# The same steps in another order: a hand-written order of windowed attention and a gated feed-forward block

## The chip, the core and the metric

The kernel runs on one core of a Trainium2 chip. The core has a matrix engine (TensorE, PE in the profile), three engines for element-wise work (VectorE, DVE; ScalarE, ACT; GpSimd, POOL), and SyncE (SP), which issues transfers. Each engine works through its own queue in the order in which the program gave it work, and waits for other engines by semaphores. PE writes only into PSUM, eight banks of 128 partitions by 2 KB; ACT and DVE read the banks. Transfers between device memory and on-chip memory are issued from the queues of SP, ACT and POOL. The metric is the device time of one execution in microseconds, us.

## What is computed

Attention over 4 batches of 8 heads, 768 positions and 64 values a head, with a window of 96 positions, 8 global keys and a bias that falls with the distance; its output, as 3072 tokens of 512 values, goes through a gated feed-forward block of width 1536:

```python
scores = scale * np.matmul(q, k.transpose(0, 1, 3, 2))
keep = is_global | is_local
bias = -slopes[:, None, None] * dist[None, :, :]
scores = np.where(keep, scores + bias[None], -1000000000.0)
a = np.exp(scores - scores.max(-1, keepdims=True))
attn = np.matmul(a / a.sum(-1, keepdims=True), v)
x = attn.transpose(0, 2, 1, 3).reshape(3072, 512)
g, val = x @ w_gate, x @ w_val
out = (g / (1 + np.exp(-g)) * val) @ w_out
```

## The kernel before

The work is cut into 1092 small steps. A step is a call of one short function, written as a name and numbers, and the string ORDER (line 37) lists all of them in the order in which they are given to the engines. Nothing else sets the order: the loop on lines 667 to 669 takes one step after the other. As every engine has a queue of its own, the place of a step in ORDER decides two things: what stands ahead of it on its own engine, and which of the eight PSUM banks it gets. The functions `single` and `double` (lines 236 and 226) deal out one bank or two neighbouring banks, from a list in which `release` puts a bank at the end when, in program order, its last reader has been given out. A product that gets a bank waits on the chip until that last reader is done.

The attention of a batch b is done for pairs of heads hp (four pairs), in units u of the keys, each 120 keys wide plus the 8 global keys. Tokens go in tiles t of 384, two to a batch; the feed-forward block takes its width in 12 blocks f of 128. The names:

| step | engine | what it does (line) |
|---|---|---|
| Lf, Ld, Li | ACT or SP | load the first queries (Lf.A) and keys (Lf.S) as 32-bit numbers, the table of distances, the identity (253 to 259) |
| Lh, Lv, LG, L4, Lr, Lw, Lo | POOL | load other queries and keys, values, global values, stages of later batches, the three weights (263 to 320) |
| cast | A, V or P | the first queries and keys to 16 bits (352) |
| T, U | PE | transposes of queries (last number 1) and keys (0) of batch 0 and of batch 1 (369, 407) |
| k, q; kw, qw | A or V | copy the transposed keys and queries of batch 0 and 1 out of PSUM (382, 398; 415, 425); k and kw end with a small copy of the global keys on DVE (388, 419) |
| sl, M | DVE, ACT | the slopes times the identity (334); exp of the biases as masks (340) |
| B, c, x, m | PE, PE, ACT, DVE | the bias written into PSUM (466), scores (479), exp (489), mask (508). In batch 0 a unit gets either B ahead of c or m behind x |
| w | PE | weighted values; the last number is 0 for the denominators, 1 and 2 for the numerators (540) |
| i, r, p, n | DVE, DVE, DVE, ACT | reciprocal of the denominators, its spreading, the scaled x, the numerators out of PSUM (556, 563, 573, 549) |
| g, v | PE | the products with w_gate and w_val, four matmuls of 384 columns (590); ga and gb are the two halves of a g |
| t, s, h | ACT, DVE, DVE | tanh of half the gate, (1 + tanh) times the gate, times the value (596, 600, 606) |
| o, e | PE, ACT | the product with w_out in parts of three matmuls (631), and its way out (649), with the store issued by SP |
| D, K | SP, DVE | transposes by DMA of queries and keys of batches 2 and 3 and of half of batch 1 (435), keys into their blocks (442 to 445) |
| G, Z | V, P or S | copies of the global values, a cleared tail (282, 280, 285) |

A last letter V, A, P or S names the engine. T.3.0.1 is the transpose of the queries of head pair 3, first half; w.0.0.0.2 is batch 0, heads 0 to 3, first half, second numerator. For batch 1, hp 0 and 1 are transposed on PE (U, then kw and qw), the rest by DMA.

The second gate of waits is the buffers: two staging buffers each for keys and for queries, two for DMA-transposed keys, two for the output rows.

Of the kernel before, what the change touches and what calls it, by code (L numbers as in the profile page):

```python
# [60 lines left out]
x.1.1.1 h.1.1 o.0.0.0 v.1.11 g.1.9 v.1.9 s.1.5 v.1.5 g.1.7 t.1.7 g.1.3 t.1.9 Lr.1.1.6 m.1.0.1.V  # L61
D.1.2.1 m.1.0.0.V h.1.5 Lv.1.3 D.1.3.0 o.0.1.0 g.1.11 o.0.0.1 Lv.1.2 o.0.1.1 t.1.3 o.0.0.2 s.1.7
Lr.3.0.1 Lr.2.0.5 v.1.0 m.1.1.1.V o.0.1.2 o.0.1.3 D.1.3.1 t.1.11 s.1.9 s.1.3 s.1.11 o.0.0.3 h.1.0
v.1.3 h.1.11 m.1.1.0.V w.1.0.0.0 h.1.9 Lv.2.2 Lr.2.1.0 K.1.2 i.1.0.0 e.0.1 w.1.0.0.1 Lr.2.0.4 e.0.0
w.1.0.0.2 c.1.2.1 h.1.3 c.1.2.0 r.1.0.0 n.1.0.0 o.0.2.0 Lr.2.1.4 D.2.0.0 K.1.3 x.1.2.1 p.1.0.0.0.V
x.1.2.0 o.0.2.1 Lv.1.5 o.1.0.0 c.1.3.0 c.1.3.1 m.1.2.1.V c.1.0.2 o.0.2.2 o.1.0.1 x.1.3.0 m.1.3.0.V
# [638 lines left out]
```

## Time and profile before

| | before |
|---|---|
| runs | 239.68, 239.74, 240.7 us; median 239.74 |
| profiled execution | 239.84 us |
| its span (first to last instruction) | 238.0 us |
| PE busy | 231.6 us, 97% of the span |
| DVE busy | 171.7 us, 72% |
| ACT busy | 117.5 us, 49% |
| POOL busy | 78.2 us, 33%, all of it in the first 112 us |
| granted TensorE clock | 1.00 |

What lies around the span is 239.84 - 238.0 = 1.84 us. In rows of the timeline the first number is the start in us from the span's start, the second the length of the merged instructions, then the engine (with q: its sequencer, which issues and waits), the line, the operation, what it writes and reads, and how many were merged; in brackets stands the idle time of the engine just before and what ended it. In groups by line the numbers after the bar are busy time in us, the mean of one in ns, and the idle time before. A matmul's end is modelled, so the busy time of PE holds waits; where PE stands still is read from the distance between starts.

### The profile page before, as it was taken

Reading aid. Unit: us, or ns where it says so; the run is one execution under the profiler, and the core shown is the slowest. Engines: PE = TensorE matmul, PEld = TensorE weight load, DVE = VectorE, ACT = ScalarE, POOL = GpSimd, SP = SyncE. Lnnn points to the kernel's source line nnn. Section 1 sums busy time; section 2 is a strip of 40 time slices with the busy share of each in tenths; the row PEclk is TensorE's granted clock in tenths of the full one; section 3 lists DMA queues with packets and bytes.
Section 4 is the critical chain, followed back from the end, with each engine's and each line's share of the span. In section 5 each row is a group of like instructions: output and inputs, shape, how many; then the busy total and the mean of one; then the engine's idle time right before and its main releaser. Section 6 shows DMA issues by size and latency. Waiting matters only on the chain.

```text
span 238.0 us, 5798 instructions
## 1 busy us (share of the span) xinstructions
PE 231.6 (97%) x2356; PEld 133.7 (56%) x2356; DVE 171.7 (72%) x411; ACT 117.5 (49%) x218; POOL 78.2 (33%) x99
## 2 busy tenths in 40 slices
PE   6999999999999999999999999999999999999994
PEld 4566566554556555555655654665555655555452
DVE  3799999767799976877948879889548854755400
ACT  3799813943776336377543366632453414223111
POOL 8874896720799845776000000000000000000000
PEclk9999999999999999999999999999999999999999
DMA  7999999999999999999974060100020101100114
GB/s 167 177 185 206 192 194 177 183 183 135 182 145 155 151 148 148 168 167 128 134 113 104 30 86 17 74 3 0 3 88 0 47 4 48 41 0 27 64 45 176
DMA packets 88715, 25.56 MB, mean 107 GB/s; under 512 B 78536, under 2 KB 85744, under 8 KB 88688
## 3 DMA queue, kind: packets, MB, share of 16 engines
q0 software_dynamic: 67520, 13.81, 70.9%
q1 hardware_dynamic: 20480, 10.80, 24.1%
q10 hardware_dynamic: 688, 0.59, 0.7%
q8 instruction: 18, 0.29, 0.6%
q14 instruction: 9, 0.07, 0.1%
HBM read 28.58 MB, written 6.29 MB: 146 GB/s over the span
## 4 chain that ended last, share of the span: by engine, by line
PE 89%; DMA 4%; ACT 3%; DVE 1%; issue 0%; SPq 0%; DVEq 0%; ACTq 0%
PE banks L590 52%; PE banks L631 25%; PE banks L540 5%; PE banks L479 4%; ACT at L489 2%; DMA dist<-dist_c 2%; DMA kN<-kst 2%; PE banks L620 1%; PE banks L466 1%; PE banks L369 1%; PE banks L407 1%; DVE xT L573 0%; DVE rb L563 0%; ACT masks L340 0%; ACT qT L398 0%
## 5 line engine op out<-in xcount | busy, mean ns | idle before, releaser
L596 ACT ACTIVATE th<-banks 128x384 f32<-128x384 f32 x96 | 44.7, 493 | 71.1 <-PE banks L590 68.0
L590 PE MATMUL banks<-xT,wv 128*128 128x384 f16 x384 | 72.7, 326 | 0.1
L590 PE MATMUL banks<-xT,wg 128*128 128x384 f16 x384 | 72.3, 326 | 0.1
L631 PE MATMUL banks<-wo,hT 128*128 128x512 f16 x276 | 68.0, 379 | 0.3 <-DVE sl L600 0.3
L606 DVE TENSOR_TENSOR hT<-banks,sl 128x384 f16<-128x384 f32 x96 | 51.5, 552 | 20.9 <-PE banks L590 19.5
L600 DVE SCALAR_TENSOR_TENSOR sl<-th,banks 128x384 f32<-128x384 f32 x96 | 50.3, 546 | 16.5 <-ACT th L596 15.7
L590 PEld LDWEIGHTS <-wv 128*128 128x128 f16 x384 | 37.1, 98 | 27.8 <-issue 0.7
L590 PEld LDWEIGHTS <-wg 128*128 128x128 f16 x384 | 36.8, 98 | 26.3 <-issue 0.3
L489 ACT ACTIVATE at<-banks 128x864 f16<-128x864 f32 (+2 forms) x52 | 42.1, 842 | 9.2 <-PE banks L479 8.6
L631 PEld LDWEIGHTS <-hT 128*128 128x128 f16 x276 | 26.1, 98 | 27.5 <-issue 1.5
L508 DVE TENSOR_TENSOR at<-at,masks 128x864 f16<-128x864 f16 (+3 forms) x60 | 25.5, 470 | 3.9 <-ACT at L489 3.7
L267 POOL DMA_DIRECT2D vS<-in_v_dram x28 | 25.4, 914 | 7.0 <-DMA vS<-in_v_dram 2.3
L649 ACT ACTIVATE osb<-banks 128x512 f32<-128x512 f32 x23 | 13.5, 598 | 25.0 <-PE banks L631 23.4
L308 POOL DMA_DIRECT2D kst<-in_k_dram x20 | 17.1, 855 | 16.7 <-PE banks L540 12.1
L308 POOL DMA_DIRECT2D qst<-in_q_dram x20 | 17.0, 858 | 3.6 <-DMA wo<-in_moe_w_out_dram 1.0
L479 PE MATMUL banks<-qT,kT 64*128 64x216 f16 (+5 forms) x240 | 14.4, 240 | 0.0
L573 DVE TENSOR_TENSOR xT<-ns,rb 128x384 f16<-128x384 f32 x24 | 12.6, 548 | 0.1
L479 PEld LDWEIGHTS <-kT 64*128 64x128 f16 x240 | 8.3, 94 | 7.4 <-issue 5.9
L540 PE MATMUL banks<-at,vS 128*32 128x216 f16 (+6 forms) x576 | 12.0, 225 | 0.4 <-issue 0.4
L549 ACT COPY ns<-banks 128x768 f32<-128x768 f32 x12 | 9.6, 799 | 4.8 <-PE banks L540 4.7
L540 PEld LDWEIGHTS <-vS 128*32 128x32 f16 x576 | 9.8, 95 | 2.6 <-issue 2.2
L556 DVE STREAM_TRANSPOSE dT<-banks 128x384 f32<-128x384 f32 x16 | 9.2, 575 | 1.4 <-PE banks L540 1.2
(59 smaller groups left out, 116.5 us busy)
## 6 DMA issues: line engine op xcount, KB each, us to landing
out_dram<-osb SPq DMA_DIRECT2D x23, 256.0 KB, 2.2
vS<-in_v_dram POOLq DMA_DIRECT2D x24, 120.0 KB, 7.6
qst<-in_q_dram POOLq DMA_DIRECT2D x20, 96.0 KB, 8.1
kst<-in_k_dram POOLq DMA_DIRECT2D x20, 96.0 KB, 7.4
wg<-in_moe_w_gate_dram POOLq DMA_DIRECT2D x6, 256.0 KB, 9.2
wv<-in_moe_w_val_dram POOLq DMA_DIRECT2D x6, 256.0 KB, 8.9
wo<-in_moe_w_out_dram POOLq DMA_DIRECT2D x3, 512.0 KB, 8.6
q<-in_q_dram POOLq DMA_DIRECT2D x3, 192.0 KB, 7.0
```

Of the source, the lines that this page charges most:

```text
L267: nc.gpsimd.dma_start(out=v_of(b)[NG:NG + n, c, :, :], in_=v[b, :, KC * c:KC * c + n, :].rearrange("h p d -> p h d"))
L308: nc.gpsimd.dma_start(out=rows_of(i, b, h // 2)[:, :, h % 2, :], in_=KQ[i][b, h].rearrange("(t p) d -> p t d", p=128))
L479: nc.tensor.matmul(sc[:, hi, col:col + n], lhsT=kTs[hp][r, 128 * c:128 * c + 128], rhs=qTs[b, hp][r, q0:q0 + n], start=fresh, stop=True, s ...
L489: nc.scalar.activation(out=at[:, :, 0:w], in_=scs.pop((b, hp, u))[:, :, 0:w], func=AF.Exp, scale=scale)
L508: ENG[e].tensor_mul(a2, a2, m[:, :, m0:m0 + n])
L540: nc.tensor.matmul(dst[r, o:o + n], lhsT=vSs[b][:, c, 4 * g + j, what - 1::2] if what else ones[:, 0:32], rhs=ats[b, hp, u][:, j % 2, col: ...
L590: nc.tensor.matmul(gv[t, f, which][:, 0:TB], lhsT=w[:, c, 128 * f:128 * f + 128], rhs=xTs[t][:, c, :], start=(c == 0), stop=(c == NC - 1))
L596: nc.scalar.activation(out=th, in_=gv[t, f, 0][:, 0:TB], func=AF.Tanh, scale=0.5)
L600: nc.vector.scalar_tensor_tensor(out=sl, in0=gv[t, f, "t"], scalar=1.0, in1=gv[t, f, 0][:, 0:TB], op0=AluOp.add, op1=AluOp.mult)
L606: nc.vector.tensor_mul(hTs[t][:, f, :], gv[t, f, 1][:, 0:TB], gv[t, f, "s"])
L631: nc.tensor.matmul(ops_t[t, i], lhsT=hTs[t][:, f, 128 * i:128 * i + 128], rhs=wo[:, f, :], start=(f == 0), stop=(f == NFF - 1))
L649: nc.scalar.mul(out=osb, in_=ops, mul=0.5)
```

## The change

All 1092 steps stay, but for six, which change their engine or their unit:

| before | after | |
|---|---|---|
| cast.0.1.A | cast.0.1.V | first keys of head pair 1: ACT to DVE |
| cast.0.0.A | cast.0.0.P | first keys of head pair 0: ACT to POOL |
| kw.0.V | kw.0.A | keys of batch 1, pair 0: DVE to ACT |
| qw.1.V | qw.1.A | queries of batch 1, pair 1: DVE to ACT |
| B.0.1 | B.0.2 | bias by PE for unit 2 in place of unit 1 |
| m.0.0.2.V | m.0.0.1.V | mask by DVE for unit 1 in place of unit 2 |

All others stand at another place. The table of distances (Ld.S) is first on SP's queue, ahead of the identity and the keys. Ten of the sixteen mask steps M stand at the head of ACT's queue, ahead of the first copy (before, they stood among the exps). The casts of the keys leave ACT. On POOL's queue cast.0.0.P stands between the loads Lh.1.1.0.4 and Lh.0.1.0.4, and Z.0.P and G.0.4.7.P stand earlier. On PE's queue T.3.0.1 and T.2.0.1 stand ahead of the first scores, T.3.1.0 stands ahead of w.0.0.0.2, and the four U of batch 1 are followed by five v, with all four copies out of their banks on ACT. The steps of later batches are mixed anew; among them K.3.3, before the last of the four K.3, comes first.

The diff is one hunk, 89 lines against 89, and only ORDER differs. Its first fourteen lines on each side, and those around the places that the prediction speaks of:

```diff
@@ -35,89 +35,89 @@
 ORDER = """
-Lf.A.1.1 Lf.S.0.1 LG pre cast.1.1.V fill.14 Li T.1.0.1 Lf.A.1.0 sl.3 cast.0.1.A sl.2 T.1.0.0 Ld.S
-B.1.0 Lf.S.0.0 B.1.1 k.1.0.V Lh.1.0.4.8 sl.1 cast.1.0.V fill.2 q.1.0.V cast.0.0.A sl.0 sl.6 sl.5
-T.0.0.1 c.0.1.1 T.0.0.0 c.0.1.0 M.3.1 T.3.0.1 T.2.0.1 q.0.0.A x.0.1.1 B.0.0 Lh.0.0.4.8 k.0.0.V B.0.1
-sl.4 c.0.0.1 sl.7 q.3.0.V M.5.1 Lv.0.2 M.0.1 Lh.1.1.0.4 Lv.0.0 x.0.1.0 c.0.0.0 q.2.0.V T.2.0.0
-x.0.0.1 T.3.0.0 k.2.0.V B.3.0 M.2.1 B.2.0 x.0.0.0 c.0.2.0 Lh.0.1.0.4 B.2.1 M.1.1 k.3.0.V w.0.0.0.0
-c.0.3.0 x.0.2.0 T.1.1.0 Z.2.V Lh.1.1.4.8 T.1.1.1 c.0.2.1 x.0.3.0 G.0.1.4.V i.0.0.0 q.1.1.V T.0.1.1
-B.3.1 c.0.3.1 T.0.1.0 Lv.0.3 k.1.1.A q.0.1.V k.0.1.V Lv.0.1 Lh.0.1.4.8 x.0.2.1 r.0.0.0 Lw.0.0.0
-T.3.1.1 T.2.1.1 x.0.3.1 q.3.1.A c.0.1.3 c.0.0.2 w.0.1.0.0 i.0.1.0 Lw.0.0.1 q.2.1.A w.0.0.0.1
-Lw.1.0.1 x.0.0.2 w.0.0.0.2 Lw.1.0.0 c.0.0.3 Lw.0.1.1 T.3.1.0 Lw.0.1.0 p.0.0.0.1.V r.0.1.0 T.2.1.0
-Lw.1.1.0 x.0.1.3 x.0.0.3 Z.0.P p.0.0.0.0.V w.0.1.0.1 p.0.1.0.0.V w.0.1.0.2 p.0.1.0.1.V k.3.1.A
-Lw.1.1.1 c.0.1.2 k.2.1.A ga.0.2 Lv.0.6 ga.0.0 ga.0.1 c.0.2.2 x.0.1.2 gb.0.0 m.0.0.2.V M.7.1 gb.0.1
-Lw.0.2.0 x.0.2.2 t.0.0 m.0.1.3.V m.0.1.2.V g.0.3 t.0.1 Lw.0.2.1 M.1.0 gb.0.2 m.0.0.3.V c.0.3.3 t.0.3
-c.0.3.2 s.0.0 t.0.2 Lv.0.5 s.0.1 w.0.0.1.0 v.0.0 M.4.1 s.0.3 s.0.2 v.0.2 v.0.3 h.0.0 M.5.0 M.6.1
-h.0.2 Lv.0.4 v.0.1 m.0.2.2.V x.0.3.3 Lw.1.2.1 c.0.2.3 x.0.3.2 x.0.2.3 M.2.0 g.0.7 m.0.3.3.V i.0.0.1
...
-Lr.1.1.7 m.0.3.2.V v.0.5 v.0.7 r.0.0.1 v.0.4 g.0.9 t.0.6 t.0.5 s.0.7 s.0.5 s.0.6 L4.1.0 h.0.5 Z.3.P
...
-t.1.1 g.1.2 s.0.10 v.1.8 g.1.4 h.0.4 h.0.10 s.0.8 s.1.1 U.0.0 U.1.1 t.1.8 U.0.1 U.1.0 t.1.2 s.1.8
-Lo.1 qw.0.A s.1.2 Lr.1.0.5 Lr.1.1.5 g.1.6 M.4.0 h.1.8 v.0.9 kw.0.V qw.1.V M.6.0 M.7.0 v.1.2 g.1.0
-kw.1.A h.0.9 h.1.2 t.1.4 v.1.6 M.0.0 t.1.6 c.1.0.1 t.1.0 s.1.4 s.1.6 c.1.1.0 x.1.1.0 D.1.2.0 Z.1.V
-g.1.5 G.1.0.7.S v.1.4 s.1.0 t.1.5 x.1.0.1 v.0.8 h.1.4 h.1.6 c.1.0.0 c.1.1.1 Lo.2 h.0.8 v.1.1 x.1.0.0
...
-w.2.1.1.0 w.2.1.1.2 i.2.0.1 c.3.1.1 c.3.0.1 D.3.3.0 o.3.2.0 i.2.1.1 x.3.0.1 K.3.2 g.4.7 n.2.1.1
-o.3.2.1 K.3.3 t.4.7 v.4.1 r.2.1.1 s.4.7 x.3.1.1 v.4.7 c.3.0.0 D.3.2.1 c.3.1.0 h.4.7 h.4.1 o.3.0.0
...
+Lf.A.1.1 Ld.S Lf.A.1.0 M.2.0 pre Li cast.1.1.V sl.0 sl.2 LG Lh.1.0.4.8 Lf.S.0.1 M.3.1 fill.14 sl.4
+M.6.0 sl.5 Lh.0.0.4.8 Lf.S.0.0 Lv.0.0 T.1.0.1 cast.0.1.V M.2.1 sl.3 B.1.1 Lh.1.1.0.4 cast.0.0.P
+q.1.0.V T.1.0.0 cast.1.0.V M.5.1 B.1.0 Lh.0.1.0.4 Z.0.P M.1.0 M.0.1 M.4.0 fill.2 sl.1 T.0.0.1 M.1.1
+M.7.1 T.0.0.0 k.1.0.V sl.7 Lv.0.3 k.0.0.V q.0.0.A M.5.0 T.3.0.1 T.2.0.1 c.0.1.1 Lh.1.1.4.8 Lv.0.2
+c.0.1.0 B.0.0 q.2.0.V q.3.0.V T.2.0.0 x.0.1.1 x.0.1.0 c.0.0.1 c.0.0.0 T.3.0.0 x.0.0.1 k.2.0.V B.2.0
+Lv.0.1 B.2.1 x.0.0.0 Lh.0.1.4.8 c.0.2.1 c.0.2.0 x.0.2.0 M.0.0 x.0.2.1 Lw.0.0.0 M.7.0 M.6.1 T.1.1.1
+k.3.0.V m.0.0.1.V sl.6 Lw.0.0.1 q.1.1.V T.0.1.1 T.0.1.0 Z.1.V Lw.1.0.1 k.0.1.V Lw.1.0.0 T.1.1.0
+B.3.0 c.0.3.0 B.3.1 Lw.0.1.0 c.0.3.1 x.0.3.0 q.0.1.V w.0.0.0.0 x.0.3.1 T.2.1.1 B.0.2 Lw.0.1.1
+G.0.1.4.V G.0.4.7.P k.1.1.A Lv.0.6 Lw.1.1.0 w.0.1.0.0 i.0.0.0 i.0.1.0 c.0.0.2 r.0.0.0 q.2.1.A
+c.0.1.3 w.0.0.0.1 T.3.1.1 x.0.0.2 T.3.1.0 x.0.1.3 r.0.1.0 k.3.1.A c.0.0.3 p.0.0.0.0.V w.0.0.0.2
+w.0.1.0.1 p.0.0.0.1.V p.0.1.0.0.V w.0.1.0.2 Lw.1.1.1 x.0.0.3 T.2.1.0 q.3.1.A ga.0.1 c.0.1.2
+p.0.1.0.1.V ga.0.2 ga.0.0 Lw.0.2.0 x.0.1.2 gb.0.2 m.0.1.3.V gb.0.0 m.0.0.3.V k.2.1.A t.0.2 m.0.1.2.V
+gb.0.1 t.0.0 c.0.2.2 c.0.3.2 Lw.0.2.1 s.0.2 x.0.2.2 w.0.0.1.0 s.0.0 t.0.1 g.0.3 v.0.0 Lv.0.5 x.0.3.2
+t.0.3 i.0.0.1 s.0.1 h.0.0 M.4.1 c.0.3.3 c.0.2.3 v.0.2 x.0.2.3 Lv.0.4 x.0.3.3 r.0.0.1 Lw.1.2.0 v.0.1
+g.0.5 g.0.6 g.0.4 h.0.2 g.0.7 v.0.5 Lw.1.2.1 m.0.2.2.V t.0.6 Lr.1.1.4 s.0.3 h.0.1 m.0.2.3.V v.0.3
+t.0.5 v.0.7 L4.1.0 m.0.3.3.V s.0.5 L4.0.0 Lv.1.2 v.0.6 m.0.3.2.V h.0.5 s.0.6 g.0.9 Lo.1 Lr.2.0.1
...
+s.0.11 g.1.1 h.0.4 D.1.2.0 s.0.10 g.1.0 t.0.8 v.0.11 g.1.8 s.0.9 U.1.1 h.0.10 Z.2.V s.0.8 t.1.2
+U.0.0 U.1.0 s.1.2 U.0.1 Lr.1.0.6 h.0.11 v.1.1 t.1.1 s.1.1 v.1.8 t.1.0 G.1.0.7.S t.1.8 qw.0.A
+Lr.1.0.7 D.1.2.1 v.1.0 kw.1.A Lr.1.1.7 qw.1.A h.1.1 s.1.8 D.1.3.0 Lr.3.0.1 v.1.2 kw.0.A v.0.8 h.1.8
+Lv.1.5 Lr.2.1.3 g.1.6 Lr.2.1.1 g.1.5 h.1.2 s.1.0 c.1.1.0 h.0.8 t.1.6 c.1.0.1 g.1.4 x.1.1.0 s.1.6
...
+t.4.6 s.4.3 h.3.11 o.2.1.2 s.4.6 t.4.4 m.2.2.2.V g.4.5 v.3.9 g.4.2 g.4.10 v.4.6 h.3.9 K.3.3 g.4.1
...
 """
```

More of the change, by code (lines that the diff above doesn't have):

```diff
@@ L61 @@
[L61 to L66, printed above, removed]
@@ new lines @@
+i.1.1.0 o.1.0.1 r.1.1.0 Lr.2.1.5 n.1.1.0 Lr.2.0.7 o.1.0.2 x.1.0.2 D.2.1.0 Lr.2.1.4 Lr.2.1.6 x.1.3.2
+c.1.2.2 c.1.1.2 v.1.10 p.1.1.0.0.V p.1.1.0.1.V K.2.0 h.1.10 g.2.0 g.2.7 m.1.0.2.V g.2.6 D.2.2.0
+x.1.2.2 x.1.1.2 t.2.0 Lr.3.0.3 g.2.3 o.1.0.3 t.2.6 g.2.5 s.2.0 t.2.7 Lr.2.1.7 D.2.0.1 m.1.3.2.V
+s.2.6 t.2.5 v.2.6 m.1.2.2.V s.2.7 e.1.0 m.1.1.2.V s.2.5 v.2.0 w.1.1.1.0 w.1.1.1.1 D.2.1.1 Lv.2.3
+t.2.3 s.2.3 w.1.1.1.2 Z.3.P w.1.0.1.2 n.1.1.1 i.1.1.1 w.1.0.1.0 w.1.0.1.1 n.1.0.1 g.2.10 i.1.0.1
+v.2.3 g.2.2 v.2.2 t.2.2 h.2.3 h.2.6 D.2.2.1 h.2.0 g.2.1 t.2.10 Lv.3.1 Lv.2.0 g.2.9 o.1.1.0 Lr.3.1.1
@@ new lines @@
+s.3.1 Lv.3.6 Lv.3.3 Lr.3.0.4 v.3.0 g.3.0 v.2.8 t.3.0 h.3.8 g.3.5 s.3.7 h.2.8 s.3.0 c.2.1.0 c.2.0.2
+D.3.3.0 t.3.5 x.2.1.0 v.3.7 s.3.5 x.2.0.2 h.3.0 v.3.3 h.3.7 g.3.9 c.2.1.1 h.3.3 m.2.1.0.V c.2.2.1
+c.2.2.0 o.2.2.0 x.2.2.0 K.2.3 m.2.0.1.V t.3.9 o.2.2.1 D.3.1.0 v.3.5 x.2.1.1 s.3.9 D.3.0.1 m.2.2.0.V
+Lv.3.4 x.2.2.1 g.3.10 g.3.4 c.2.3.1 t.3.4 c.2.3.0 x.2.3.1 h.3.5 s.3.4 m.2.2.1.V g.3.11 o.2.2.2
+o.2.0.0 m.2.1.1.V x.2.3.0 t.3.11 Lr.3.0.0 o.2.0.1 t.3.10 m.2.3.0.V g.3.2 o.2.2.3 v.3.1 s.3.11 t.3.2
+m.2.3.1.V e.2.2 w.2.1.0.2 s.3.2 w.2.1.0.1 w.2.0.0.0 w.2.1.0.0 h.3.1 w.2.0.0.1 w.2.0.0.2 n.2.1.0
@@ new lines @@
+h.4.0 h.4.5 v.4.3 v.4.2 s.4.2 w.2.1.1.1 w.2.1.1.2 e.3.1 h.4.3 s.4.8 h.4.2 K.3.0 w.2.1.1.0 w.2.0.1.2
+D.3.1.1 n.2.1.1 w.2.0.1.1 w.2.0.1.0 c.3.0.0 K.3.2 o.3.2.0 n.2.0.1 x.3.0.0 i.2.0.1 g.4.7 t.4.7
+i.2.1.1 c.3.0.1 c.3.1.0 r.2.1.1 c.3.1.1 s.4.7 p.2.1.1.1.V o.3.2.1 r.2.0.1 x.3.1.1 x.3.0.1 x.3.1.0
+o.3.2.2 o.3.0.0 o.3.2.3 m.3.1.1.V m.3.0.1.V e.3.2 p.2.0.1.0.V o.3.0.1 c.3.3.0 c.3.2.1 c.3.2.0
+o.3.0.2 G.3.0.7.S Lv.3.0 m.3.0.0.V x.3.2.0 p.2.1.1.0.V Lv.3.2 v.4.1 p.2.0.1.1.V v.4.10 v.4.7 x.3.2.1
+h.4.1 m.3.1.0.V g.4.11 w.3.0.0.2 x.3.3.0 h.4.10 t.4.11 m.3.2.1.V w.3.0.0.1 c.3.3.1 m.3.3.0.V x.3.3.1
@@ new lines @@
+o.3.0.3 n.3.0.0 g.5.10 g.5.0 v.4.8 m.3.2.0.V m.3.3.1.V t.5.10 g.4.9 e.3.0 s.4.11 g.5.11 t.5.0 s.5.10
+s.5.0 t.4.9 t.5.11 h.4.8 h.4.7 g.5.3 t.5.3 v.5.10 h.5.10 s.4.9 w.3.1.0.2 w.3.1.0.1 w.3.0.0.0
+w.3.1.0.0 g.5.7 v.5.0 n.3.1.0 g.5.4 i.3.0.0 v.4.11 g.5.2 s.5.11 i.3.1.0 h.5.0 h.4.11 t.5.7 s.5.3
+v.5.3 r.3.1.0 v.5.7 g.5.9 s.5.7 t.5.2 s.5.2 g.5.8 o.4.2.0 h.5.3 v.5.11 v.4.9 t.5.4 t.5.9 h.5.7 v.5.2
+v.5.9 r.3.0.0 t.5.8 p.3.1.0.0.V s.5.9 s.5.8 h.4.9 o.4.2.1 o.4.2.2 s.5.4 g.5.1 p.3.0.0.0.V
+p.3.0.0.1.V h.5.11 t.5.1 o.4.2.3 h.5.9 g.5.6 e.4.2 p.3.1.0.1.V t.5.6 h.5.2 c.3.0.2 c.3.1.2 x.3.0.2
@@ L121 @@
+h.7.10 v.7.3 o.5.0.1 o.6.2.0 o.6.0.2 h.7.5 o.6.0.3 t.7.8 s.7.3 v.7.11 o.5.0.2 h.7.3 o.6.1.3 o.7.0.0
+e.6.0 v.7.6 s.7.8 v.7.8 o.5.0.3 h.7.11 v.7.7 h.7.6 h.7.7 o.7.0.1 e.5.0 o.6.2.1 o.7.1.0 h.7.8 o.7.2.0
+o.6.2.2 e.6.1 o.7.0.2 o.6.2.3 e.6.2 o.7.0.3 e.7.0 o.7.2.1 o.7.1.1 o.7.1.2 o.7.1.3 o.7.2.2 e.7.2
+o.7.2.3 e.7.1 e.7.3
 """
```

90 lines of the change are left out of this document (34 added, 56 removed).

## The prediction

> **What bounds the kernel now.** The page came first. Lines of its parts 1 and 2:
>
> ```profile
> span 238.0 us, 5798 instructions
> PE 231.6 (97%) x2356; PEld 133.7 (56%) x2356; DVE 171.7 (72%) x411; ACT 117.5 (49%) x218; POOL 78.2 (33%) x99
> PE   6999999999999999999999999999999999999994
> DMA  7999999999999999999974060100020101100114
> ```
>
> PE has work from the first us to the last, at a granted clock of 1.00. The reader is to see two things: only the waits of PE can be shortened, since its work stays; and the transfers fill their engines for the first half of the span, so what a load has ahead of it sets when it lands. Second came the waits of PE: none that it lists behind the first 20 us is over 0.3 us. So, third, I took the distances between starts from the timeline, and the end of PE from the chain of waits (start, length, what):
>
> ```profile
> 1.19 3.17 PE L348 MATMUL banks<-ones 128*128 128x256 f16 x14 [1.19 <-DVE ones L326]
> ...
> 42.58 1.46 PE L590 MATMUL banks<-xT,wv 128*128 128x384 f16 x8
> 43.88 0.81 PE L590 MATMUL banks<-xT,wg 128*128 128x384 f16 x4
> 44.69 0.81 PE L590 MATMUL banks<-xT,wv 128*128 128x384 f16 x4
> 45.43 0.54 PE L479 MATMUL banks<-qT,kT 64*128 64x216 f16 x8
> ...
> 233.85 0.68 PE banks L620 x12
> ```
>
> From 42.58 to 43.88 eight matmuls of 384 columns take 1.30 us: 0.1625 each, 0.42 ns a column, 0.65 for one g or v. From 43.88 to 44.69 four take 0.81 instead of 0.65, so a wait of 0.16 sits in a stretch that the page calls busy. From 44.69 to 45.43 four take 0.74: the 0.09 over 0.65 is the change from matmuls on the whole array to those on part of it. With 0.42 ns a column (the small matmuls side by side) and 0.09 a change, the PE work of the old order adds up to 228.4 us. It ran from 1.19 to 233.85 + 0.68 = 234.53, 233.3 us. So all that a better order could win is 4.9 us: 4.2 before the first g, 0.7 behind it.
>
> **The change part by part.**
>
> *PE's own work.* The steps are the same but for B.0.2 in place of B.0.1: 192 more columns, 0.08 us. Changes of the array's shape, counted in the two orders: 86 before, 87 after, 0.09. Together +0.17, with no cover, since PE is the bound.
>
> *The start.* Rows of the timeline of before, then two groups by shape, then two lines of the page's part 6 (KB each, median us to landing):
>
> ```profile
> 0.74 0.46 SPq L259 DMA_DIRECT2D k<-in_k_dram  x1
> 1.75 0.43 SPq L256 DMA_DIRECT2D dist<-dist_c  x1
> 3.91 0.51 ACT L352 CAST k<-k 128x384 f16<-128x384 f32 x1 [0.83 <-DMA k<-in_k_dram]
> 2.17 0.79 POOL L263 DMA_DIRECT2D q<-in_q_dram  x1
> 4.65 0.77 POOL L263 DMA_DIRECT2D q<-in_q_dram  x1
> 6.34 0.86 POOL L263 DMA_DIRECT2D k<-in_k_dram  x1
> 7.20 0.51 ACT L352 CAST k<-k 128x384 f16<-128x384 f32 x1 [2.78 <-DMA k<-in_k_dram]
> 8.51 0.46 ACT L489 ACTIVATE at<-banks 128x336 f16<-128x336 f32 x1
> 9.21 0.84 PE L369 MATMUL banks<-ident,q 128*64 128x128 f16 x12
> 10.07 0.78 POOL L263 DMA_DIRECT2D k<-in_k_dram  x1
> 17.87 0.56 DVE L573 TENSOR_TENSOR xT<-banks,rb 128x384 f16<-128x384 f32 x1 [0.38 <-ACT at L489]
> 19.41 1.14 PE L590 MATMUL banks<-xT,wg 128*128 128x384 f16 x6
> ...
> L340 ACT ACTIVATE masks<-dist 128x432 f16<-128x432 f16 x8 | 4.5, 574 | 0.0
> L340 ACT ACTIVATE masks<-dist 128x216 f16<-128x216 f16 x8 | 2.9, 386 | 0.0
> ...
> q<-in_q_dram POOLq DMA_DIRECT2D x3, 192.0 KB, 7.0
> k<-in_k_dram POOLq DMA_DIRECT2D x3, 192.0 KB, 7.2
> ```
>
> ACT sits idle for 2.78 us ahead of the second cast. Ten masks move into such idle time; six long and four short, 6 x 4.5/8 + 4 x 2.9/8 = 4.8 us, from about 4 on. But the keys of pair 1 change places with the table on SP, first issue against third: they landed at 3.9, the time at which the first cast could start, and now land near 6. And the first scores stand behind T.3.0.1 and T.2.0.1, which ran at 9.21, when their queries had landed (issued at 2.17, 7.0 to landing). So the first exp moves from 8.51 to about 9.9. From there ACT has fewer masks between its exps up to x.0.1.3: one long and two short (1.3 us) instead of four long ones (2.25); x.0.1.3 ends near 18.3 instead of 17.85, where the row at 17.87 shows DVE waiting for it. Then T.3.1.0 waits for the last load ahead of the weights (issued at 10.07 before, 7.2 to landing: 17.3), w.0.0.0.2 stands behind it, and r and p, about 0.5 each (that p took 0.56), behind that. The first g starts at 19.5 to 20.0 instead of 19.41.
>
> POOL's queue gets a hole: cast.0.0.P waits for the keys of pair 0 (7.2, the start of the second cast), and behind it wait all later loads. Its own price is not in the trace. Rows near it:
>
> ```profile
> 27.57 1.65 POOL L282 COPY vS<-vG 8x1536 f16<-8x1536 f16 x1
> ...
> 12.98 0.88 DVE L282 COPY vS<-vG 8x1536 f16<-8x1536 f16 x1
> ...
> 6.55 0.35 DVE L352 CAST q<-q 128x384 f16<-128x384 f32 x1
> ```
>
> By the elements of a row POOL would take 384/1536 of 1.65, 0.4 us; at most the whole 1.65. By POOL's ratio to DVE it is 1.65/0.88 times the cast's 0.35, 0.7: that I take, as the ratio is of one and the same copy. So POOL issues nothing from 5.4 (4.65 + 0.77) to 7.9, and the load that was issued at 6.34 comes 1.6 us later. What hides this is the backlog: the load issued at 4.65 lands 7.0 later, at 11.7, so the transfer engines have work through the hole. If that cover is gone, up to 2.5 us, the hole's length, are paid once. By the Trainium skill, DMA: Bandwidth & Descriptors, section "Issuing engines are not separate DMA queues", all issuers feed the same engines, and issue time is usually small beside the transfer; by that rule the hole costs nothing, and the trace agrees as far as this backlog goes.
>
> Then the weights set the pace, which is why a quicker start would not help:
>
> ```profile
> L315 POOL DMA_DIRECT2D wg<-in_moe_w_gate_dram x1: 700/700/700, 21.3 to 21.3; - x1
> DMA to landing us min/median/max: 10.2/10.2/10.2
> ...
> 31.47 1.46 PE L590 MATMUL banks<-xT,wg 128*128 128x384 f16 x8
> ```
>
> The last gate weight lands at 21.27 + 10.18 = 31.45, and g.0.9, the first that needs it, starts at 31.47. The new order has the same bytes ahead of this load, so I leave its landing at 31.45; but it brings g.0.9 after seven v instead of eight. PE reaches it 0.6 us of work too early, if it starts the products as early as before; if it starts up to 0.6 later, the delay is used up in that wait. Either way PE is 0.55 us behind. Bounds: -0.4 (first g at 19.0 and loads 1 us earlier) to +2.0 (1.5 of the hole comes through).
>
> *The hand-over of batch 1.* The four copies kw and qw, and the two small DVE copies that end kw:
>
> ```profile
> 41.69 0.80 ACT L425 COPY qT<-banks 128x768 f16<-128x768 f16 x1 [1.38 <-PE banks L407]
> ...
> 43.22 0.85 ACT L415 COPY kT<-banks 128x720 f16<-128x720 f16 x2
> ...
> 44.00 0.34 DVE L419 COPY kT<-kT 128x56 f16<-128x56 f16 x1 [0.52 <-ACT kT L415]
> 44.09 1.01 DVE L606 TENSOR_TENSOR hT<-banks,sl 128x384 f16<-128x384 f32 x2
> ```
>
> Here lies the wait of 0.16: DVE waits 0.52 for ACT's kw.1, h.0.9 and h.1.2 are queued behind the small copy, and v.1.6 needs h.0.9's bank. Afterwards ACT does all four in the order qw.0, kw.1, qw.1, kw.0, and qw.0 waits for the last U. Counted from the end of the U: qw.0 starts at 0.2 and kw.1 at 0.9 (from 41.69 on, qw held ACT 0.70), kw.1 is done at 1.75, qw.1 at 2.45, kw.0 at 3.3. On DVE h.1.1 stands behind kw.1's small copy: done at 2.4. v.1.2 gets the bank of h.1.1 and would start at 0.1 + 3 x 0.65 = 2.05: a wait of 0.35. Then h.1.8 stands behind kw.0's small copy: done at 3.95; g.1.6 gets its bank and would start at 2.4 + 1.3 = 3.7: 0.25. Together 0.6 for 0.16, +0.45. Lower end 0 (the two copies that leave DVE let it catch up), upper 1.0, if the 0.5 that DVE waited here comes on top.
>
> *Waits that go.* Two later ones:
>
> ```profile
> 140.73 0.35 DVE L442 COPY kT<-kN 128x720 f16<-128x720 f16 x1 [1.49 <-DMA kN<-kst]
> ...
> 142.22 1.46 PE L631 MATMUL banks<-wo,hT 128*128 128x512 f16 x6 [0.32 <-DVE sl L600]
> ...
> 122.17 1.73 PE L590 MATMUL banks<-xT,wv 128*128 128x384 f16 x8
> ...
> 123.74 0.81 PE L590 MATMUL banks<-xT,wg 128*128 128x384 f16 x4
> ```
>
> K.3.3 waited 1.49 us for its transpose, the s behind it was late, and PE stood 0.32. With K.3.3 first of the four, its transpose is issued far ahead of its use. From 122.17 to 123.74 eight matmuls take 1.57 instead of 1.30: 0.27, a bank that an output row on ACT held. The new order puts other steps there. Together -0.6. What is late next I can't name for all 215 us; along the SP queue each D has some us of room, the least (by my count of the steps between issue and use, 0 to 1) for K.3.0 and for D.3.1.1, which stands behind the store of e.3.1. I set +0.25 for the new waits, with bounds 0 and 1.2 (twice what the old order had). So -0.35.
>
> *The end.* The last steps of PE, the last output rows and their stores stand as before: 0.
>
> *The sum*, against the profiled execution of 239.84: +0.17 + 0.55 + 0.45 - 0.35 = +0.82, 240.66. That execution stands 0.10 above the median of the runs shown, 239.74; so 240.6 for the median.
>
> **The rivals.**
>
> *The hole starves the transfers.* The cast waits for a load that is itself behind others, takes up to 1.65, and the engines run dry; each weight then lands later and PE waits at g.0.9. The price is 1.5 to 2.5 beyond the sum: 242.1 to 243.1. For it: the DMA row of the page is full from the second slice on, so time lost there isn't won back. Against it: the backlog of 11.7 - 7.9 = 3.8 us. It decides from a landing of the last gate weight later than 32.3 on. By the Trainium skill, SBUF — State Buffer, section "SBUF: two separate sides", a copy or cast between SBUF places on DVE keeps POOL from writing its descriptors, which speaks against the second cast that DVE gets. The trace shows little of it: the load issued at 6.34, across the cast at 6.55, took 0.86 us on POOL, the one at 4.65 0.77 and the one at 10.07 0.78.
>
> *The masks were the start's bound (the other side: faster).* The row at 17.87 speaks for it: p waits for an exp, and masks stood among the exps. If c.0.1.1 is not held, ACT's stream from the first exp on is shorter by 2.25 - 1.3 = 0.95, the first g comes at 18.5, and the weights land a us earlier, since the holes in POOL's queue fill differently. Then start -0.7, hand-over +0.3, waits -0.6, work +0.17: 238.9. With no hand-over wait and all the 0.7 behind the first g won as well it is 238.3. It decides when the last gate weight lands before 30.4.
>
> *A transpose comes late.* D.3.1.1 or K.3.0 misses its place, PE waits up to 1 us near 138: 241.3 to 241.6. For it: 1.49 us of such a wait in before; against it: room of 0 to 1 us in the new order.
>
> *Nothing comes of it.* The hand-over wait is covered, and gains and losses cancel: 239.7 to 240.0.
>
> **How the numbers follow.** About 0.5% (1.2 us) is what a measurement of this kernel can tell from no change. The forecast, 240.0 to 241.2, has 0.45: 0.35 of it within 0.5% of 239.74 (up to 240.94), 0.10 above. The starved transfers 0.25, all slower. A late transpose 0.08, slower. Nothing 0.10, same. The faster rival 0.12: 0.09 beyond 0.5%, 0.03 within. So faster 0.09, same 0.48, slower 0.43. The range reaches from 239.2, which leaves out the faster rival, to 242.6, the middle of the starved case.
>
> **What would show it.** PE: the first g between 19.4 and 20.0, a distance larger than its work just ahead of the matmuls that first read the last gate weight, waits of 0.2 to 0.5 on DVE's h in the 3 us behind the U, and no PE wait behind K near 140. POOL: a cast of 0.4 to 1.1 that starts at 7.2, no issue for 2.5 us. The prediction is wrong if the weights land more than 0.9 us later or 1 us earlier than 31.45, or if a wait that I could not name, over 1 us, stands behind 46 us.

## The result, and the profile after

The changed kernel takes 241.83 us (median of 10 runs, 241.31 to 242.7), the kernel before 240.09 beside it: ratio 1.0074, 95% interval 1.0047 to 1.0102. Measured once more on another chip it was 1.0100 (1.0073 to 1.0127). So it is slower, by 1.1 to 2.4 us; 0.82 was forecast. The profiled execution took 241.45 us, 1.61 more than the one of before.

From the page of the changed kernel, parts 1 and 2:

```profile
span 239.7 us, 5802 instructions
PE 231.5 (97%) x2356; PEld 133.0 (55%) x2356; DVE 170.5 (71%) x409; ACT 119.3 (50%) x219; POOL 78.2 (33%) x100
PE   6989999999999999999999999999999999999994
PEclk9799999999999999999999999999999999999999
DMA  7999999999999999999923352100101011010124
```

PE is as busy as before in a span that is 1.7 us longer. The third digit of its row is an 8 instead of a 9: part of the loss is in the first 20 us. The second digit of PEclk is a 7: the clock granted to PE was at half for a part of that time, which the last section takes up. The chain of waits of the changed kernel says which work held the end there, and where it leaves PE later (start, length, what; a piece begins where the one ahead of it ends, so it can begin some hundredths after its instruction):

```profile
2.17 5.25 DMA k<-in_k_dram
...
7.47 0.50 POOL k L352
7.97 0.72 POOL k L263
8.69 0.32 POOL vS L285
9.01 0.87 POOL vS L267
9.88 0.76 POOL q L263
10.64 1.84 POOL vS L267 x2
12.47 6.11 DMA k<-in_k_dram
...
18.62 0.36 PE banks L369 x6
...
20.48 0.43 PE banks L590 x2
...
43.21 0.77 ACT kT L415
...
44.10 0.56 DVE hT L606
...
137.08 4.22 DMA qT<-qst
```

It has three places. From 2.17 to 18.62 it is not PE but the cast on GpSimd, the five issues queued behind it (with the cleared tail Z.0.P, L285, among them), and the last key load, which T.3.1.0 waits for. At 43 to 44 it is kw.1 and the h behind it, at 137.08 the transpose D.3.1.1. In the timeline of the changed kernel (PE, DVE and SP):

```profile
20.41 0.50 PE L590 MATMUL banks<-xT,wg 128*128 128x384 f16 x2
...
31.95 1.46 PE L590 MATMUL banks<-xT,wg 128*128 128x384 f16 x8
...
44.70 1.46 PE L590 MATMUL banks<-xT,wv 128*128 128x384 f16 x8 [0.17 <-DVE hT L606]
...
141.35 0.54 PE L479 MATMUL banks<-qT,kT 64*128 64x216 f16 x8 [0.55 <-DMA qT<-qst]
...
44.01 0.18 DVE L419 COPY kT<-kT 128x56 f16<-128x56 f16 x1 [2.39 <-ACT kT L415]
...
136.62 0.33 SPq L650 DMA_DIRECT2D out_dram<-osb  x1
137.08 1.34 SPq L435 DMA_TRANSPOSE qT<-qst  x1
```

The first g is at 20.41 instead of 19.41: 1.00 of the 1.64 us by which the span grew. From the first g to the start of PE's last matmul it is 215.48 us, 214.89 before: 0.59. Measured by the distances between starts, over the work and the shape changes, PE's waits in that stretch are:

| wait of PE | before | after |
|---|---|---|
| hand-over of batch 1, near 44 and 46 | 0.16 | 0.33 + 0.17 |
| output row on ACT, 122.66 | 0.27 | - |
| s behind K.3.3, 141.65 | 0.39 | - |
| D.3.1.1, 140.55 | - | 0.71 |
| near 149, a copy of global values | - | 0.13 |
| two of less than 0.1 | 0.13 | - |
| sum | 0.95 | 1.34 |

That is 0.39; the other 0.20 is PE's own work. The end adds 0.05.

### The profile page after: what moved, and what is told of

Read it like the earlier page. It is cut to its first block, busy times and chain, and to the rows that moved or that the text cites. A ratio compares the mean times of both kernels' runs of the same rounds, so it can differ in the third digit from the quotient of the medians.

```text
span 239.7 us, 5802 instructions
## 1 busy us (share of the span) xinstructions
PE 231.5 (97%) x2356; PEld 133.0 (55%) x2356; DVE 170.5 (71%) x409; ACT 119.3 (50%) x219; POOL 78.2 (33%) x100
## 4 chain that ended last, share of the span: by engine, by line
PE 88%; DMA 6%; POOL 2%; SPq 1%; issue 1%; DVE 0%; ACT 0%
PE banks L590 52%; PE banks L631 25%; PE banks L540 5%; DMA k<-in_k_dram 5%; PE banks L479 4%; DMA qT<-qst 2%; POOL vS L267 1%; PE banks L620 1%; PE banks L407 1%; ACT kT L415 0%; POOL q L263 0%; POOL k L263 0%; PE banks L369 0%; DVE hT L606 0%; SPq L259 0%
## 5 line engine op out<-in xcount | busy, mean ns | idle before, releaser
L596 ACT ACTIVATE th<-banks 128x384 f32<-128x384 f32 x96 | 45.2, 492 | 71.8 <-PE banks L590 66.8
L600 DVE SCALAR_TENSOR_TENSOR sl<-th,banks 128x384 f32<-128x384 f32 x96 | 51.3, 545 | 15.0 <-ACT th L596 14.4
L489 ACT ACTIVATE at<-banks 128x864 f16<-128x864 f32 (+2 forms) x52 | 41.2, 836 | 10.1 <-PE banks L479 10.0
L508 DVE TENSOR_TENSOR at<-at,masks 128x864 f16<-128x864 f16 (+5 forms) x60 | 26.1, 469 | 4.2 <-ACT at L489 4.0
L479 PE MATMUL banks<-qT,kT 64*128 64x216 f16 (+4 forms) x240 | 14.4, 241 | 0.5 <-DMA qT<-qst 0.5
```

What stands on the lines that cost most here:

```text
L479: nc.tensor.matmul(sc[:, hi, col:col + n], lhsT=kTs[hp][r, 128 * c:128 * c + 128], rhs=qTs[b, hp][r, q0:q0 + n], start=fresh, stop=True, s ...
L489: nc.scalar.activation(out=at[:, :, 0:w], in_=scs.pop((b, hp, u))[:, :, 0:w], func=AF.Exp, scale=scale)
L508: ENG[e].tensor_mul(a2, a2, m[:, :, m0:m0 + n])
L596: nc.scalar.activation(out=th, in_=gv[t, f, 0][:, 0:TB], func=AF.Tanh, scale=0.5)
L600: nc.vector.scalar_tensor_tensor(out=sl, in0=gv[t, f, "t"], scalar=1.0, in1=gv[t, f, 0][:, 0:TB], op0=AluOp.add, op1=AluOp.mult)
```

## The experiments

The edits stand against the changed kernel or the kernel before, as said at each. The loss lies in the start and behind the first g, so I first mended the three places one by one and together. Times are medians; the ratio is to the kernel before, run on the same chip in the same minutes.

**The cast back on ScalarE** (of the changed kernel), which takes the wait out of GpSimd's queue:

```diff
-... B.1.1 Lh.1.1.0.4 cast.0.0.P
+... B.1.1 Lh.1.1.0.4
-M.7.1 T.0.0.0 ...
+M.7.1 cast.0.0.A T.0.0.0 ...
```

> The changed kernel with the cast of the first keys of head pair 0 on ScalarE, behind mask M.7.1, instead of on GpSimd: GpSimd's queue has no wait in it. Changed kernel 241.8, its first g at 20.41, last gate weight at 31.78. Theory A (the wait in GpSimd's queue made the last key load late, 18.58 instead of 17.37, and the transpose T.3.1.0 hands that on to the first g; the weights then set the pace): first g at 19.3 to 19.7, last gate weight near 31.45, PE waits 0.3 to 0.6 us in front of g.0.9, time 241.0 to 241.5. Rival B (the weights come earlier by as much as the loads ahead of them): last gate weight near 30.6, no wait at g.0.9, time 240.6 to 240.9. Rival C (the masks or the late keys of pair 1 set the first g): first g stays above 20.1, time 241.6 to 241.9.

Measured 241.24, ratio 1.0071 (1.0043 to 1.0100): next to nothing won. The first g is at 20.33. The last key load lands at 17.58 and no longer holds anything, and the transfers move 169 GB/s from 11 to 14 us, where the changed kernel had 121. The chain of waits of this run shows another path, just as long:

```profile
1.60 4.94 DMA k<-in_k_dram
...
6.56 0.36 DVE k L352
...
9.40 1.42 PE banks L369 x19
...
13.83 0.89 ACT at L489
...
18.44 0.46 PE banks L369 x12
...
20.39 0.43 PE banks L590 x2
```

It begins with the keys of pair 1, third on SP's queue behind the table, and goes through PE's transposes and ACT's exps. These keys are cast at 6.56 here, at 6.03 in the changed kernel, so the length of this path is that of one execution; that next to nothing was won rests on the medians. The time is rival C's; the wait that theory A names is in the trace of the changed kernel, but taking it out alone wins nothing.

**D.3.1.1 ahead of the output row e.3.1** (of the changed kernel):

```diff
-... w.2.1.1.2 e.3.1 h.4.3 ... w.2.0.1.2
-D.3.1.1 n.2.1.1 ...
+... w.2.1.1.2 D.3.1.1 e.3.1 h.4.3 ... w.2.0.1.2
+n.2.1.1 ...
```

> The changed kernel with D.3.1.1, the transpose by DMA of the queries of batch 3, pair 1, ahead of the output row e.3.1 whose store stood in front of it on SP's queue. Theory A (the store holds the transpose back, and PE's wait of 0.71 at 140.55 is that alone): it is issued near 133.4 instead of 137.08, no PE wait over 0.1 between 139 and 143, time 241.1. Rival: something else is as late (the keys of batch 3, or a wait on ScalarE or VectorE right behind): over 0.4 of the 0.71 is left, or stands within 3 us behind it, time 241.6 or more.

Measured 240.87, ratio 1.0051 (1.0022 to 1.0079). The timeline of this run, SP and then PE:

```profile
133.55 1.23 SPq L435 DMA_TRANSPOSE qT<-qst  x1
136.68 0.34 SPq L650 DMA_DIRECT2D out_dram<-osb  x1
...
140.51 0.73 PE L479 MATMUL banks<-qT,kT 64*128 64x216 f16 x12
```

It is issued ahead of the store, and the scores that stood still for 0.55 run through. The wait was the store in front, as theory A has it. Behind the first g this run takes 214.84 instead of 215.48, so it won the 0.64 there.

**The small copies of kw as steps of their own, later** (of the changed kernel):

```diff
 def keys_whole(hp, e):
...
-        nc.vector.tensor_copy(
-            out=k3[:, :, 0:NG],
-            in_=k3[:, 0, NG:2 * NG].unsqueeze(1).broadcast_to([128, NCH, NG]))
         release((1, hp, 0))
+    def keys_global(hp):
+        k3 = chunked(hp)
+        nc.vector.tensor_copy(
+            out=k3[:, :, 0:NG],
+            in_=k3[:, 0, NG:2 * NG].unsqueeze(1).broadcast_to([128, NCH, NG]))
-... qw.1.A h.1.1 s.1.8 ... v.0.8 h.1.8
+... qw.1.A h.1.1 kz.1 s.1.8 ... v.0.8 h.1.8 kz.0
```

> The changed kernel with the small VectorE copies of the global keys that end kw.1 and kw.0 as steps of their own, behind h.1.1 and h.1.8. Theory A (h.1.1 and h.1.8 stand behind copies that wait for ScalarE): PE's waits of 0.33 at 44.20 and 0.17 at 45.83 go, time 241.3. Rival (VectorE is simply behind with its work there, 0.5 us of products late whatever stands in front): more than 0.3 of the 0.5 is left, time 241.6 to 241.9.

Measured 240.91, ratio 1.0054 (1.0034 to 1.0075). Both waits at 44 and 46, 0.50 together, are gone from the trace. What PE waits behind the first g falls from 1.34 to 0.65, by more than these, since the wait for D.3.1.1 is shorter in this execution too (0.30 where PE stood still for 0.55). Theory A holds.

**All three together**:

> All three edits together. If the three waits are independent, the gains add: 0.5 (start, by theory A with the weights' pace) + 0.7 (late transpose) + 0.5 (small copies) = 1.7, time 240.1, level with the kernel before. By rival B at the start 1.0 + 0.7 + 0.5 = 2.2, time 239.6. If a wait that was hidden behind these comes up, less than 1.2 is won: 240.6 or more.

Measured 239.54, ratio 1.0013 (0.9993 to 1.0034): level with the kernel before, as the independent sum said, although that sum had 0.5 for the start, of which the first edit alone had won next to nothing. First g at 19.58 in this execution, PE's waits behind it 0.35.

**PE kept busy at the start** (of the kernel with all three):

```diff
-... T.1.0.1 cast.0.1.V M.2.1 sl.3 B.1.1 ...
+... T.1.0.1 sl.3 cast.0.1.V M.2.1 B.1.1 fill.4 ...
-... M.4.0 fill.2 sl.1 ...
+... M.4.0 sl.1 ...
```

> The kernel with all three edits (239.5 beside 239.5 for before), and at the start slope sl.3 ahead of the cast of the keys of pair 1 on VectorE, and fill.2 made fill.4 and put behind B.1.1, into the time in which TensorE waits for those keys. Theory D (in the changed order TensorE idles from 5.2 to 6.6, its rate halves from 8 to 11 as the profile's clock row shows, and the chain of transposes and first scores that sets the first g runs at half rate): the clock stays at 1.00 from 7 to 12, 128-column transposes in that stretch at about 0.06 us instead of 0.11, first g at 18.8 to 19.2 instead of 19.6. Then the weights' pace shows: PE reaches g.0.9 about 11.4 behind the first g, at 30.2 to 30.6, with the last gate weight at 31.0 to 31.5, so waits of 0.5 to 1.0 in front of weights, time 239.2 to 239.5. If the weights do not set the pace, 238.7 to 239.0. Rival (the start is set by the key load or the exps, whatever TensorE's rate): first g at 19.5 or later, time 239.5 to 239.8.

Measured 239.29, ratio 0.9993 (0.9969 to 1.0018), not to be told from the kernel it was built on. Its profiled execution, one of its longest (240.68), had the first g at 20.78, and its chain of waits has the transposes no quicker than in the other runs of this start:

```profile
8.95 1.42 PE banks L369 x22
```

The fills did not bring a quicker rate in this execution, and the median is no better. Theory D is neither shown nor refuted: what a start at full rate would win was not seen here.

**The cast on GpSimd, alone, in the kernel before**:

```diff
-... q.1.0.V cast.0.0.A sl.0 ... B.0.0 Lh.0.0.4.8 ... Lv.0.2 M.0.1 Lh.1.1.0.4 Lv.0.0
+... q.1.0.V Lh.0.0.4.8 Lv.0.2 Lh.1.1.0.4 cast.0.0.P sl.0 ... B.0.0 ... M.0.1 Lv.0.0
```

> The kernel before with one part of the change alone: the cast of the first keys of pair 0 on GpSimd, behind the fifth of its loads, as in the changed kernel. By the prediction's rival of starved transfers: 1.5 to 2.5 more than before, 241.5 to 242.5. By what the changed kernel shows (the loads behind the wait land 1.2 later, the last gate weight 0.3 later, and here T.3.1.0 stands behind w.0.0.0.2, so that the late key load does not hold the first g): first g at 19.4 to 19.8, last gate weight at 31.7 to 32.0, PE waits 0.2 to 0.5 in front of g.0.9, 0.2 to 0.6 more than before. If the wait costs nothing at all: within 0.2 of before.

Measured 238.93, ratio 0.9970 (0.9951 to 0.9989): not slower, if anything faster, so all three expectations missed, and the starved transfers most of all. The profiled execution (239.98, a long one of its 12) shows the same wait, cast at 8.05 and a load of queries held until 16.72, with the first g at 20.38, 0.97 later than before. But its time is only 0.14 longer, for behind the first g PE takes 0.61 less than before. Two waits of before have shrunk. Near 123 it is the one of 0.27 (timeline of this run):

```profile
123.15 1.46 PE L590 MATMUL banks<-xT,wv 128*128 128x384 f16 x8
124.45 0.81 PE L590 MATMUL banks<-xT,wg 128*128 128x384 f16 x4
```

Eight matmuls take 1.30 here, where before took 1.57. Near 142 the eight scores and the wait behind them take 0.50 instead of 0.86. So this start can cost 1 us in an execution, and the time need not show it. What shrinks these waits, and why the median is lower, is open.

**The table first on SP, alone, in the kernel before**:

```diff
-Lf.A.1.1 Lf.S.0.1 LG ... fill.14 Li T.1.0.1 ... T.1.0.0 Ld.S
+Lf.A.1.1 Ld.S LG ... fill.14 Li Lf.S.0.1 T.1.0.1 ... T.1.0.0
```

> The kernel before with another part of the change alone: on SP's queue the table of distances first, then the identity, then the keys of pair 1, as in the changed kernel; all else as before. Theory E (the late keys of pair 1 are what holds the changed start even where GpSimd does not wait): these keys land near 6.0 instead of 3.9, their cast on ScalarE starts there, the transposes and first scores behind it come 0.6 to 1.2 later, first g at 20.0 to 20.6 instead of 19.4 to 19.9, time 0.4 to 0.9 over before. Rival (the table that lands at 6.0 is as late for the biases, so the two only change places): first g at 19.9 or earlier, time within 0.3 of before.

Measured 241.11, ratio 1.0060 (1.0025 to 1.0095). The chain of waits of this run has the keys in front and PE nearly all the way:

```profile
1.60 4.82 DMA k<-in_k_dram
...
6.43 0.52 ACT k L352
...
20.47 1.10 PE banks L590 x6
```

Keys cast at 6.43 instead of 3.91, first g at 20.44 instead of 19.41. The time is as theory E has it: this one move costs as much at the start as the whole change does there. The first g is as late as in the run before (20.38), but here the two waits of before are both left (1.56 at 123.21, and 0.94 for the scores at 142.39), and the time of the execution is longer, 240.95 against 239.98. PE stands idle ahead of these keys, and the granted clock is 0.62 from 8 to 11 and 0.81 from 11 to 14; what the late keys cost by themselves, and what by the slower clock, was not taken apart.

**The keys on the other queue** (of the kernel with all three): the table stays first, but the keys of pair 1 come second on ScalarE's queue.

```diff
-Lf.A.1.1 Ld.S Lf.A.1.0 ... Lf.S.0.1 M.3.1
+Lf.A.1.1 Ld.S Lf.A.0.1 ... Lf.S.1.0 M.3.1
```

> The kernel with all three edits, and the first keys of pair 1 second on ScalarE's queue (1.21), the queries of pair 1, second half, third on SP's (1.61): the table stays first. Theory E: the keys land near 4.7 instead of 5.7 to 6.7, TensorE's wait for them shrinks from over 1 us to about 0.3, first g at 19.1 to 19.6 instead of 19.6 to 20.8. By the weights' pace of the prediction: last gate weight still at 31.0 to 31.5, reached 11.5 behind the first g at 30.6 to 31.1, so waits of 0.2 to 0.6 in front of weights, time 239.0 to 239.4, 0.1 to 0.4 under the kernel with all three edits. Without that pace 238.6 to 239.0. Rival (the key load from GpSimd's queue or the exps set the first g): first g stays at 19.6 or later, no gain.

Measured 238.97, ratio 0.9956 (0.9930 to 0.9982): faster than both kernels, about 1.1 us under before. The chain has the cast of the keys at 5.46 and the first g at 19.05:

```profile
5.46 0.20 DVE k L352
...
19.11 0.43 PE banks L590 x2
```

PE's waits behind the first g are 0.21. The last gate weight lands at 30.15, and nothing waits for it.

**The same swap on the changed kernel, nothing else**:

> The changed kernel with one edit only: the first keys of pair 1 second on ScalarE's queue, the queries of pair 1, second half, third on SP's. GpSimd's wait, the late transpose and the small copies stay. Theory E with theory A beside it (two chains of about the same length set the first g: the keys of pair 1 through TensorE and ScalarE, and the wait on GpSimd through the last key load and T.3.1.0): the first chain gets about 1 us shorter, the second stays, and the first g comes 1.8 behind that load's landing (17.5 to 19.1 so far), at 19.3 to 20.9; last gate weight at 31.5 to 31.9; 0.3 to 0.7 won, ratio to before 1.0045 to 1.006. If the keys of pair 1 alone set the changed start: first g at 19.1 to 19.6, 1.0 to 1.4 won, ratio 1.0015 to 1.003.

Measured 241.63, ratio 1.0095 (1.0067 to 1.0123), and the changed kernel itself beside it:

> The changed kernel as it is, once more beside the run above: first g between 20.3 and 20.9, PE waits at 44, 46 and 140 as before, ratio to before 1.005 to 1.010.

242.06, ratio 1.0100 (1.0073 to 1.0127). So the swap alone wins nothing, though the keys land at 4.63 instead of 6.21. The chain of this run, and behind it its timeline and its stretch from 17 to 21 (busy times by engine, the granted clock after POOL's count):

```profile
7.18 0.50 POOL k L352
...
12.17 6.32 DMA k<-in_k_dram
...
18.54 0.53 PE banks L369 x3
```

```profile
19.47 1.70 PE L540 MATMUL banks<-at,vS 128*32 128x216 f16 x48
```

```profile
17.00:21.00 4.00, 3.93 (x104) 2.89 (x94) 2.91 (x7) 3.16 (x7) 4.00 (x6) 0.59 1.25 204
```

GpSimd's chain is the longest, as it was in both profiled executions of the changed kernel. In this execution the granted clock was 0.59 of full speed in that stretch, where 48 matmuls took 1.70 (0.99 in the changed kernel); first g at 21.39. Set side by side, the four cases are: both delays there, 1.0074 and 1.0100; GpSimd's wait taken out, 1.0071; the late keys mended, 1.0095 (beside 1.0100); both, with the two later edits as well, 0.9956. Those two edits alone gave 0.0023 and 0.0020, so 0.0075 of the 0.0118 is left for the start. The two chains run side by side and end within a us of each other; mending one leaves the other. Both start cures without the two later edits were not run.

**Two waits out of the kernel before.** First D.3.3.0 ahead of the output row e.3.1, then that and the small copies of kw later:

```diff
-... K.3.1 w.2.0.1.2 e.3.1 ... c.3.0.1 D.3.3.0 o.3.2.0
+... K.3.1 D.3.3.0 w.2.0.1.2 e.3.1 ... c.3.0.1 o.3.2.0
...
-... v.0.9 kw.0.V qw.1.V ... h.0.9 h.1.2 t.1.4
+... v.0.9 kw.0.V kz.0 qw.1.V ... h.0.9 h.1.2 kz.1 t.1.4
```

> The kernel before with D.3.3.0, the transpose of the keys of batch 3, pair 3, ahead of the output row e.3.1 on SP's queue: the wait of 0.39 at 141.65, which the changed order does away with, taken out of before alone. If the store in front of it held the transpose back: D.3.3.0 issued by 134.5 instead of 136.54, no wait of VectorE for it, no PE wait near 141.65, 0.4 less than before. Rival (its buffer, which K.3.1 frees, holds it): issued after 135.5, the wait stays.

> The kernel before with D.3.3.0 ahead of the output row e.3.1, and with the small VectorE copies of kw.1 behind h.1.2 and of kw.0 on their own: the waits of 0.16 at 44.37 and 0.39 at 141.65 taken out of before. If both are independent of the start: no PE wait at these places, 0.2 to 0.6 under before, 238.8 to 239.2. If the hand-over of batch 1 is bound by ScalarE's copy kw.1 itself and not by what stands behind it: the wait of 0.16 stays, 0.1 to 0.4 under before.

Measured 239.77, ratio 1.0005 (0.9982 to 1.0028), and 239.91, ratio 0.9983 (0.9949 to 1.0018). In the traces the waits at 141.65, and in the second kernel also at 44.37, are gone; their 0.39 and 0.55 us are 0.16% and 0.23%, less than the intervals. The second kernel's profiled execution shows what the reader should look for, the products at 43.80 and 44.45 a plain 0.65 apart, where before had 0.81:

```profile
43.80 0.81 PE L590 MATMUL banks<-xT,wg 128*128 128x384 f16 x4
44.45 0.81 PE L590 MATMUL banks<-xT,wv 128*128 128x384 f16 x4
```

## Why the prediction was right in direction and short in size

- *PE's own work*, +0.17: 0.20 behind the first g. Right.
- *The start*, +0.55: 1.00 in the profiled executions. Three steps of it were wrong:
  - "What hides this is the backlog" failed. The load issued at 4.64 landed at 11.12, somewhat ahead of the 11.7 reckoned, but the values behind the hole landed at 14.93, 2.74 behind the load ahead of them, and the last key load at 18.58 instead of 17.37. In the stretch from 11 to 14 the transfers (last number, GB/s) moved a third less; the busy times by engine of that stretch, of before and then of the changed kernel:

```profile
11.00:14.00 3.00, 3.00 (x57) 1.86 (x56) 2.60 (x9) 3.00 (x6) 2.17 (x4) 1.00 1.90 176
```

```profile
11.00:14.00 3.00, 2.81 (x57) 2.00 (x54) 2.81 (x12) 2.29 (x4) 3.00 (x5) 0.94 1.37 121
```

  That is 3 x 55 = 165 KB, about 0.9 us at the rate of before. From the rule of the Trainium skill, DMA: Bandwidth & Descriptors, section "Issuing engines are not separate DMA queues", that issue time is usually small beside the transfer, the prediction read a price of zero; but the rule speaks of issuing, not of a queue that stands still, and here the measured 1.2 at the last key load decides. The cast itself took 0.50, against 0.7 taken and 0.4 to 1.65 as bounds, and was issued and waited for as forecast (7.47, nothing issued from 5.42 to 7.93).
  - "The keys of pair 1 change places with the table" was seen and priced too low. The first exp came at 9.49, even before the 9.9 reckoned. I let the missing masks win most of that back (x.0.1.3 near 18.3; it ended at 18.76), and never priced PE's own chain of transposes and biases behind those keys. Alone in before, this move cost 0.6%.
  - "The weights set the pace" failed. g.0.9 was to wait for the last gate weight and take in whatever the start lost. In the changed kernel the weight, issued at 22.75, lands 9.03 later at 31.78, and PE gets to g.0.9 at 31.95: no wait. The row of that load, from the groups by line:

```profile
L315 POOL DMA_DIRECT2D wg<-in_moe_w_gate_dram x1: 698/698/698, 22.8 to 22.8; - x1
...
DMA to landing us min/median/max: 9.0/9.0/9.0
```

  In the run with the keys on the other queue the first g came at 19.05 and the weight at 30.15, still without a wait. What looked like a pace at 31.45 and 31.47 was a landing just in time. The timeline of before shows it already: sixteen matmuls start at 28.87, and at 0.1625 each, 2.60, they fill PE up to 31.47.

```profile
28.87 2.76 PE L590 MATMUL banks<-xT,wv 128*128 128x384 f16 x16
```

  The 0.55 rested on this pace. Without it the prediction's own first g, 19.5 to 20.0, gives 0.1 to 0.6. So the direction of the start was right, by that first g, and the size had no ground.
- *The hand-over*, +0.45: 0.33 + 0.17 - 0.16 = 0.34. Right in mechanism and size: DVE waits 2.39 for ACT's kw.1 with h.1.1 behind it, and the waits go when the small copies are moved.
- *Waits that go*, -0.35: both forecast ones went, and two small ones, -0.79. But the unknown new ones, set at +0.25, are 0.84, of which D.3.1.1 is 0.71. So the term is +0.05.
- *The rivals.* The late transpose came true at the place named, with 0.71 where up to 1 was said, and I had given it 0.08. The starved transfers came in part: they moved a third less for 3 us, but the weights land 0.33 later, not 0.9 or more, and in before that wait costs nothing in the median. The faster rival rested on masks as the bound; the start was bound by other things. What the Trainium skill, SBUF — State Buffer, section "SBUF: two separate sides", says of casts on DVE and the descriptors of POOL could not be tried: GpSimd had nothing to issue while DVE cast these keys, from 6.03 to 6.39.

The sum by measured terms: 0.20 + 1.00 + 0.34 + 0.05 + 0.05 at the end = 1.64, the growth of the span. The predicted 240.6 and the measured 241.83 differ by this, 0.8 us, and by the kernel before, which stood at 240.09 beside it instead of 239.74. The forecast ended at 241.2, so the measured time lies beyond it. That it still lies in the range is luck: the upper end, 242.6, came from the starved transfers at their full price, which was not paid. By the bound of 0.5% the change is slower, to which 0.43 was given, against 0.48 for no difference.

## What to carry to other kernels

Where a start is held by a load, ask for the second-longest chain before pricing a cure: here two chains of equal length, one through GpSimd's queue and one through the first keys, hid each other, so that each cure alone gave nothing, and with both (and the two later edits) the first g came at 19.05 instead of 20.41 to 21.23. A wait on a queue that issues loads is to be priced by the last load behind it that somebody waits for; in the changed kernel that was the key load, 1.2 late, while the weights were 0.33 late and held nothing. And a transpose by DMA behind a store in one queue is late by whatever the store waits for: list, for every one, what stands directly in front of it.
